# Linear attention in units of one whole load group, with the maxima in the bank of the key-value sums

## The chip, the cores and the metric

The kernel runs on one core of a Trainium2 chip. The metric is the device time of one execution in microseconds (us), from a launch with all inputs in device memory. PE is TensorE, DVE is VectorE, ACT is ScalarE, POOL is GpSimd and SP is SyncE.

## The reference

Three parts follow each other: a linear attention with positive random features, a gated MLP with an RMS norm ahead of it, and a second MLP.

```
scale = 1 / sqrt(sqrt(D))                      # D = 64, m = 128 features
phi(x): proj = x*scale @ omega.T               # q, k, v: batch 4, heads 8, seq 576, D 64
        h = proj - sum((x*scale)^2)/2
        exp(h - max(h)) / sqrt(m)
kv = phi(k).T @ v ;  z = sum(phi(k))           # per batch and head
attn = (phi(q) @ kv) / (phi(q) @ z + 1e-6)
x = attn as 2304 tokens x 512
xn = x / rms(x) * rms_g
x = (silu(xn @ w_gate) * (xn @ w_val)) @ w_out # d_ff 1536
out = silu(x @ w_in) @ w_out2                  # d_ff 2048
```

The MLP weights arrive as float64 words, which the kernel turns into float32 itself.

## The kernel before

A float32 product is made of three passes on TensorE: each operand is split into a high part (a rounded copy, made by ScalarE) and a low part (the rest, a subtraction on VectorE), and `PASS` runs high*high, high*low and low*high.

**Attention.** A load group is 256 rows of four heads of k or q in one tile `x` of 128 partitions x 512 (row pairs, so four heads x two rows = eight columns of 64); a tail group holds the last 64 rows of two batches and is half as wide. There are 32 whole groups and 8 tail groups. A whole group is worked on as two units of four columns, one after the other; with the tails there are 72 units. Each unit runs through the same steps, named here as in the code: `tr` (PE, L586: two transposes into a PSUM buffer `b`), `tr_hi` (ACT, L592) and `tr_lo` (DVE, L595), which split the transposed tile into `hl`, `pj` (PE, L605: six matmuls against `bd`, the features), `mx` (DVE, L620: the maximum over the features of four columns, into `small`), `top` and `nb` (DVE, L626 and L633: the bias of the exponential from the maximum and the squared norms `ns`), and `ex` (ACT, L644: four exponentials into `e`). A k unit then adds its part of the key-value sums (`kv`, PE, L690); after the last one of a batch and a half of the heads VectorE copies the sums to `kvs` (L710). A q unit is transposed again (`fl`, L721, and `ev` on ACT, L727), multiplied with `kvs` (`num`, L736), divided on VectorE (`den`, `rec`, `mu`, L759 to L772), and when a tile of 128 tokens is whole it is normed (`ss` on ACT, `rstd` on POOL, `xn` on DVE, L833), transposed (`xf`, L842) and split into `xs` (`x_hi`, `x_lo`, L851 and L856).

**PSUM.** The eight banks are: one for `small` (maxima and intermediate sums of three units), one for the key-value sums `kv`, and six buffers `b` for everything else.

**Weights.** Each weight tile is loaded into `raw`, decoded in five steps on VectorE and two on POOL, and split (`w_hi`, `w_lo`). The first six and three more are prepared during the attention, the others later.

**The order.** The attention, the weights of the first sweep and the first sweep of the gated MLP over the first three blocks of tokens (`part`, L236, into `b`; `out`, L963) are written as `Op`s with an engine, an estimated duration, dependences and buffers that they claim and free. `run_order` (L413) is a list scheduler: it takes again and again the operation that can start earliest, with `RANK` added to a place in the sequence as priority. So the table `RANK`, the durations and the buffer counts in `SLOTS` set the order in which the instructions stand on each engine; the engines then run their own instructions strictly in that order and wait for each other by semaphores that the framework sets from the tiles that instructions touch. After `run_order`, `stream` writes the rest of the MLPs in a fixed order (L236, L290, L323), and every few microseconds of estimated TensorE work a `tick` puts in the next step of a weight.

Of the kernel before, what the change touches and what calls it, by code (L numbers as in the profile page):

```python
# [20 lines left out]
def kernel(  # L21
# [202 lines left out]
    W_EARLY, GRAIN = 3, 3  # L224
# [152 lines left out]
    class Op:  # L377
# [15 lines left out]
        "ld_om": 41.7, "t_om": -211.5, "s_om": -232.3, "bd_hi": -107.5, "bd_lo": 58.9,  # L393
# [4 lines left out]
        "rstd": -389.4, "xn": 36.2, "xf": -367.8, "x_hi": -48.8, "x_lo": 225.6, "ld_w": 11.5,  # L398
        "w_dec": 310.2, "w_add": 254.1, "w_hi": 67.9, "w_lo": 196.9, "part": 226.4, "tanh": 300.8,
        "silu": -31.9, "glu": 10.3, "h_hi": -176.1, "h_lo": -143.8, "out": 711.2, "ya": -190.5,  # L400
    }
    SLOTS = {
# [68 lines left out]
    small = ps_a.tile([P, SLOTS["nb"], 2 * G], F32, tag="small", name="small", bufs=1)  # L471
# [25 lines left out]
    def k_units(b):  # L497
        for g in range(2):
            for hf in range(2):
                for hp in range(2 * g, 2 * g + 2):  # L500
                    yield "k", b, hf, hp, g
            if b % 2 == 0:
                yield "kt", b, 0, 0, g

    def q_units(b):
        for hf in range(2):
            for hp in range(4):
                yield "q", b, hf, hp, hp // 2
        if b % 2:
            for g in range(2):  # L510
                yield "qt", b - 1, 0, 0, g
# [8 lines left out]
    last_use = {}  # L520
    for i, (kind, b, hf, hp, g) in enumerate(units):
        last_use[kind, b, hf, g] = i
    last_k = max(i for i, u in enumerate(units) if u[0][0] == "k")
# [5 lines left out]
    def add_load(u, i):  # L529
# [42 lines left out]
    def add_unit(i):  # L572
        kind, b, hf, hp, g = units[i]
        u = kind, b, hf, g
        tail = len(kind) == 2
        if u not in ld:
            add_load(u, i)
        w = ld[u]
        st = State()

        def transposes(o):
# [18 lines left out]

        def project(o):
            st.ps = buf(ps_a, [P, G, P], "b", o.slot["b"])
            for j in range(2):
                for n, (a, c) in enumerate(PASS):
                    nc.tensor.matmul(  # L605
                        out=st.ps[:, 2 * j:2 * j + 2, :].rearrange("p h m -> p (h m)"),
                        lhsT=st.hl[:, c, j, :],
                        rhs=bd[:, a, :],
                        start=(n == 0),
                        stop=(n == 2),  # L610
                    )

        pj = Op("pj", "PE", 0.71, project, [lo] + bd_ops, i, ["b", "pjc"], [(tr, "hl")])
        pj_ops.append(pj)

        def maxima(o):
            n = o.slot["nb"]
            st.mx, st.top = small[:, n, 0:G], small[:, n, G:2 * G]
            st.nb = buf(wk, [P, G], "nb", n)
            nc.vector.tensor_reduce(out=st.mx, in_=st.ps, axis=AX.X, op=ALU.max)  # L620
            st.ns = w.ns if tail else w.ns[:, 4 * (hp % 2):4 * (hp % 2) + 4]

        mx = Op("mx", "DVE", 0.6, maxima, [pj], i, ["nb"])
        top = Op(
            "top", "DVE", 0.13,
            lambda o: nc.vector.scalar_tensor_tensor(  # L626
                out=st.top, in0=st.ns, scalar=half, in1=st.mx, op0=ALU.mult, op1=ALU.add
            ),
            [mx, w.nsop], i,
        )  # L630
        nb = Op(
            "nb", "DVE", 0.13,
            lambda o: nc.vector.scalar_tensor_tensor(  # L633
                out=st.nb, in0=st.ns, scalar=half, in1=st.top, op0=ALU.mult, op1=ALU.subtract
            ),
            [top], i, free=[(w.sqop, "ns")] if last_use[u] == i else [],
        )
        res = f"et{g}" if kind == "kt" else "e"

        def exps(o):  # L640
            pool = kp if kind == "kt" else wk
            st.e = buf(pool, [P, G, M], res, o.slot[res])
            for h in range(G):
                nc.scalar.activation(  # L644
                    out=st.e[:, h, :], in_=st.ps[:, h, :], func=AF.Exp, bias=st.nb[:, h:h + 1]
                )

        ex = Op("ex", "ACT", 1.004, exps, [nb], i, [res], [(pj, "b"), (pj, "pjc"), (mx, "nb")])
        if kind[0] == "k":
            add_kv(i, st, ex)  # L650
        else:
            add_q(i, st, ex)

    def add_kv(i, st, ex):
        kind, b, hf, hp, g = units[i]
        u = kind, b, hf, g
        va = vld[u]
        odd = b % 2
        first = kind == "k" and hf == 0 and hp % 2 == 0
        end = (hf == 1 and hp % 2 == 1) if odd else kind == "kt"  # L660
        deps = [ex, va.op, kvprev.get((b, g))]
        free = []
        if kind == "kt":
            ktexp[b, g] = st, ex, va
        else:
            free.append((ex, "e"))
            if last_use[u] == i:
                free.append((va.op, "v"))
# [415 lines left out]
```

## Time and profile before

| | us |
|---|---|
| median of 3 runs (lowest to highest) | 1010.03 (1009.59 to 1011.81) |
| the profiled execution | 1011.63 |
| its span, first to last instruction | 1009.8 |
| PE busy | 992.4 |
| DVE busy | 587.8 |
| ACT busy | 374.6 |
| POOL busy | 282.2 |

The profiled execution took 1.83 us more than its span, and lies 1.60 us above the median. A busy PE is not PE at its peak, because the ends of pipelined matmuls are modelled. The attention takes roughly the first 160 us, the blocks of the first sweep that `run_order` places go on to about 218 us, and the rest is `stream`.

### The profile page before, as it was taken

To read this page: it belongs to the slowest core of one execution; us is meant where nothing else is said; L and a number is where in the kernel's file an instruction comes from. 1 tells how busy PE (TensorE), PEld (TensorE's weight loads), DVE (VectorE), ACT (ScalarE), POOL (GpSimd) and SP (SyncE) were. 2 spreads that over 40 slices of the span, in tenths; PEclk is the share of its full clock that TensorE was granted. 3 is DMA by queue.
4 is the path that set the end of the run, shared out by engine and by line. 5 is a ranking of instruction groups with operands and counts; after the bars stand their busy time and mean duration, and the time that the engine had idled before them with its cause. 6 is when DMAs were issued, how large, how long until landed. Compare 5 with 4: busy or idle time off the path is not lost.

```text
span 1009.8 us, 15330 instructions
## 1 busy us (share of the span) xinstructions
PE 992.4 (98%) x5935; PEld 842.4 (83%) x5935; DVE 587.8 (58%) x1289; ACT 374.6 (37%) x861; POOL 282.2 (28%) x287
## 2 busy tenths in 40 slices
PE   7999998999999999999999999999999999999998
PEld 7988886788888888888888888888888888888887
DVE  7899998837852345676332776443654544535633
ACT  6988895344221112222111334433322322322321
POOL 6756632415520002344000231321411411201300
PEclk9999999999999999999999999999999999999999
DMA  7444211212320002222000120210210210200023
GB/s 196 123 122 131 67 30 42 64 41 84 104 63 1 1 1 64 63 85 83 21 1 1 42 63 22 84 42 5 79 42 6 78 42 22 63 1 21 21 84 105
DMA packets 68729, 55.85 MB, mean 55 GB/s; under 512 B 25648, under 2 KB 62768, under 8 KB 68656
## 3 DMA queue, kind: packets, MB, share of 16 engines
q1 hardware_dynamic: 68656, 54.87, 18.4%
q8 instruction: 47, 0.77, 0.3%
q14 instruction: 26, 0.21, 0.1%
HBM read 50.14 MB, written 4.72 MB: 54 GB/s over the span
## 4 chain that ended last, share of the span: by engine, by line
PE 89%; DVE 7%; issue 1%; POOL 1%; ACT 1%; DMA 1%; SPq 0%; DVEq 0%; ACTq 0%; POOLq 0%
PE g L236 43%; PE y L323 19%; PE y L290 12%; PE b L605 4%; PE b L236 3%; PE kv L690 2%; DVE small L620 2%; PE b L963 2%; PE b L736 1%; PE b L721 1%; PE b L586 1%; DVE hl L595 1%; DVE w L183 1%; POOL m L170 1%; DVE xt L833 1%
## 5 line engine op out<-in xcount | busy, mean ns | idle before, releaser
L236 PE MATMUL g<-xs,w 128*128 128x512 f32 (+1 forms) x2256 | 467.9, 366 | 0.0
L236 PEld LDWEIGHTS g<-xs,w 128*128 128x128 f32 x2256 | 391.2, 188 | 70.1
L170 POOL TENSOR_TENSOR m<-m,raw 128x512 int32<-128x512 int32 x136 | 189.9, 1396 | 612.6 <-issue 442.6
L230 DVE TENSOR_TENSOR h<-s,h 128x512 fp32r<-128x512 f32 (+1 forms) x134 | 96.0, 717 | 185.0 <-ACT h L229 185.0
L323 PE MATMUL y<-w,h 128*128 128x512 f32 (+1 forms) x870 | 200.8, 388 | 0.0
L323 PEld LDWEIGHTS y<-w,h 128*128 128x128 f32 x870 | 162.2, 188 | 33.3
L229 ACT ACTIVATE h<-s 128x512 fp32r<-128x512 f32 (+1 forms) x134 | 78.7, 588 | 191.5 <-DVE s L259 169.5
L290 PE MATMUL y<-h,w 128*128 128x512 f32 (+1 forms) x648 | 135.6, 366 | 0.3 <-DVE w L183 0.3
L290 PEld LDWEIGHTS y<-h,w 128*128 128x128 f32 x648 | 112.1, 189 | 20.5 <-DVE w L183 0.8
L270 ACT ACTIVATE s<-g 128x512 f32<-128x512 f32 (+1 forms) x80 | 44.4, 556 | 171.0 <-PE g L236 170.9
L334 DVE TENSOR_TENSOR ya<-y,ya 128x512 f32<-128x512 f32 (+1 forms) x91 | 62.2, 684 | 57.8 <-PE y L323 56.5
L259 DVE TENSOR_TENSOR s<-s,g 128x512 f32<-128x512 f32 (+1 forms) x54 | 33.8, 627 | 84.8 <-PE g L236 84.8
L301 DVE TENSOR_TENSOR ya<-y,ya 128x512 f32<-128x512 f32 (+1 forms) x80 | 50.2, 635 | 54.3 <-PE y L290 54.1
L180 ACT ACTIVATE w<-m 128x512 fp32r<-128x512 f32 x68 | 42.7, 628 | 102.8 <-POOL m L170 102.8
L644 ACT ACTIVATE e<-b,nb 128x128 f32<-128x128 f32 x272 | 77.5, 395 | 3.7 <-DVE nb L633 3.6
L605 PE MATMUL b<-bd,hl 128*128 128x256 f32 x432 | 69.5, 300 | 1.7 <-DVE hl L595 1.1
L605 PEld LDWEIGHTS b<-bd,hl 128*128 128x128 f32 x432 | 56.8, 192 | 5.4 <-DVE hl L595 2.3
L620 DVE TENSOR_REDUCE small<-b 128x4 f32<-128x512 f32 x72 | 50.2, 697 | 6.2 <-PE b L605 2.2
L253 ACT ACTIVATE s<-g 128x512 f32<-128x512 f32 (+1 forms) x54 | 29.7, 550 | 64.1 <-PE g L236 63.9
L183 DVE TENSOR_TENSOR w<-m,w 128x512 fp32r<-128x512 f32 x68 | 52.9, 779 | 0.1
L545 POOL TENSOR_TENSOR sq<-x 128x512 f32<-128x512 f32 (+1 forms) x40 | 38.9, 982 | 36.2 <-DMA x<-in_q_dram 9.8
L549 POOL TENSOR_TENSOR sq<-sq 128x256 f32<-128x256 f32 (+2 forms) x80 | 44.4, 573 | 2.3
(69 smaller groups left out, 739.7 us busy)
## 6 DMA issues: line engine op xcount, KB each, us to landing
raw<-in_moe_w_out_dram SPq DMA_DIRECT2D x28, 512.0 KB, 3.5
raw<-in_moe_w_in_dram SPq DMA_DIRECT2D x16, 512.0 KB, 3.7
raw<-in_moe_w_gate_dram SPq DMA_DIRECT2D x12, 512.0 KB, 3.6
raw<-in_moe_w_val_dram SPq DMA_DIRECT2D x12, 512.0 KB, 3.5
x<-in_k_dram SPq DMA_DIRECT2D x16, 256.0 KB, 3.4
va<-in_v_dram SPq DMA_DIRECT2D x32, 128.0 KB, 3.3
x<-in_q_dram SPq DMA_DIRECT2D x16, 256.0 KB, 3.0
out_dram<-ya SPq DMA_DIRECT2D x15, 256.0 KB, 2.0
```

Source lines behind the costliest of these rows:

```text
L170: tt(out=mi, in0=mi, in1=(low if step == 5 else high).bitcast(I32), op=ALU.add)
L183: nc.vector.tensor_tensor(out=st.t[:, 1, :], in0=st.m.bitcast(F32), in1=st.t[:, 0, :].bitcast(F32), op=ALU.subtract)
L229: nc.scalar.activation(out=ht[:, 0, :], in_=s, func=AF.Copy)
L230: nc.vector.tensor_tensor(out=ht[:, 1, :], in0=s, in1=ht[:, 0, :].bitcast(F32), op=ALU.subtract)
L236: nc.tensor.matmul(out=ps, lhsT=w[:, a, cc * P:(cc + 1) * P], rhs=xs[j][:, c, cc, :], start=(n == 0), stop=(n == 3 * KC - 1),)
L290: nc.tensor.matmul(out=ps, lhsT=wt[1, "o", f][:, a, d * P:(d + 1) * P], rhs=hs[f][:, c, :], start=(n == 0), stop=(n == nn - 1),)
L301: nc.vector.tensor_tensor(out=y[:, d, :], in0=ps, in1=y[:, d, :], op=ALU.add)
L323: nc.tensor.matmul(out=ps, lhsT=hs[f][:, a, t * P:(t + 1) * P], rhs=wt[2, "p", f][:, c, d0:d1], start=(n == 0), stop=(n == nn - 1),)
L334: nc.vector.tensor_tensor(out=o[:, t, d0:d1], in0=ps, in1=o[:, t, d0:d1], op=ALU.add)
L605: nc.tensor.matmul(out=st.ps[:, 2 * j:2 * j + 2, :].rearrange("p h m -> p (h m)"), lhsT=st.hl[:, c, j, :], rhs=bd[:, a, :], start=(n == 0) ...
L620: nc.vector.tensor_reduce(out=st.mx, in_=st.ps, axis=AX.X, op=ALU.max)
L644: nc.scalar.activation(out=st.e[:, h, :], in_=st.ps[:, h, :], func=AF.Exp, bias=st.nb[:, h:h + 1])
```

## The change

The unit becomes the whole load group. `tr` is four transposes into one buffer `b`, `tr_hi` and `tr_lo` split all eight columns at once, and `top` and `nb` work on eight columns; `pj`, `mx` and `ex` stay as they are, twice for each group (40 groups instead of 72 units for the other steps). Both maxima are there before `top`. A `kv` operation adds the eight columns of a group, after both its exponentials. The maxima move into the bank of the key-value sums: one tile `sums` of 512 words holds the sums in its first 260 and the maxima in its last 48, and a seventh buffer `b` takes the free bank. There are four `x` buffers instead of five, two `hl` instead of three (each twice as wide), two `nmc` instead of one. The square of the norm writes its unused result into the part of `xs` that `x_lo` fills later. The first weight loads are tied to another projection (`GATE`), some durations are changed, and all of `RANK` has new values.

```diff
--- before.py
+++ after.py
-    W_EARLY, GRAIN = 3, 3
+    W_EARLY, GRAIN, GATE = 3, 3, 13
...
-        "ld_v": 152.1, "tr": -174.1, "tr_hi": -646.3, "tr_lo": -622.3, "pj": -75, "mx": 580.3,
...
+        "ld_v": 43, "tr": 112.1, "tr_hi": 191.5, "tr_lo": 4.7, "pj": -40.7, "mx": -1915.3,
...
-        "x": 5, "v": 3, "vt0": 1, "vt1": 1, "sq": 2, "ns": 6, "hl": 3, "b": 6, "pjc": 4, "nb": 3, "e": 3,
-        "et0": 1, "et1": 1, "kv": 1, "kvs": 6, "qT": 2, "nmc": 1, "xt": 2, "rs": 4,
+        "x": 4, "v": 3, "vt0": 1, "vt1": 1, "sq": 2, "ns": 6, "hl": 2, "b": 7, "pjc": 4, "nb": 3, "e": 3,
+        "et0": 1, "et1": 1, "kv": 1, "kvs": 6, "qT": 2, "nmc": 2, "xt": 2, "rs": 4,
...
-    small = ps_a.tile([P, SLOTS["nb"], 2 * G], F32, tag="small", name="small", bufs=1)
+    sums = ps_a.tile([P, 512], F32, tag="sums", name="sums", bufs=1)
+    kv_sum = sums[:, 0:G * (D + 1)].rearrange("p (h d) -> p h d", h=G)
+    small = sums[:, 512 - 4 * G * SLOTS["nb"]:].rearrange("p (n t) -> p n t", n=SLOTS["nb"])
...
-                for hp in range(2 * g, 2 * g + 2):
-                    yield "k", b, hf, hp, g
+                yield "k", b, hf, g
...
+    def add_unit(u, i):
+        kind, b, hf, g = u
         tail = len(kind) == 2
-        if u not in ld:
-            add_load(u, i)
-        w = ld[u]
+        R = 1 if tail else 2
...
-            st.pt = buf(ps_a, [P, 2, P], "b", o.slot["b"])
-            st.hl = buf(wk, [P, 2, 2, P], "hl", o.slot["hl"], F32R)
-            for j in range(2):
-                h0, n = (2 * j, 2) if tail else (2 * (hp % 2) + j, 1)
-                nc.tensor.transpose(
-                    st.pt[:, j, :], w.x[:, h0:h0 + n, :, :].rearrange("p h r d -> p (h r d)"), ident
-                )
-
-        free_x = [(w.op, "x")] if last_use[u] == i else []
-        tr = Op("tr", "PE", 0.218, transposes, [w.op, w.sqop], i - 1, ["b", "hl"], free_x)
-        hi = Op("tr_hi", "ACT", 0.264, lambda o: nc.scalar.activation(out=st.hl[:, 0], in_=st.pt, func=AF.Copy), [tr], i - 0.3)
+            st.pt = buf(ps_a, [P, 2 * R, P], "b", o.slot["b"])
+            st.hl = buf(wk, [P, 2, 4, P], "hl", o.slot["hl"], F32R)
+            for j in range(2 * R):
+                nc.tensor.transpose(st.pt[:, j, :], flat()[:, j * P:(j + 1) * P], ident)
+
+        tr = Op("tr", "PE", 0.109 * 2 * R, transposes, [w.op, w.sqop], i - 1, ["b", "hl"], [(w.op, "x")])
+        hi = Op(
+            "tr_hi", "ACT", 0.25 * R,
+            lambda o: nc.scalar.activation(out=st.hl[:, 0, 0:2 * R], in_=st.pt, func=AF.Copy), [tr], i - 0.3,
+        )
         lo = Op(
-            "tr_lo", "DVE", 0.335,
+            "tr_lo", "DVE", 0.07 + 0.265 * R,
             lambda o: nc.vector.tensor_tensor(
-                out=st.hl[:, 1], in0=st.pt, in1=st.hl[:, 0].bitcast(F32), op=ALU.subtract
+                out=st.hl[:, 1, 0:2 * R], in0=st.pt, in1=st.hl[:, 0, 0:2 * R].bitcast(F32), op=ALU.subtract
...
+            pj = Op("pj", "PE", 0.715, project, [lo] + bd_ops, i, ["b", "pjc"], [(tr, "hl")] if last else [])
+            pjs.append(pj)
+
+            def maxima(o, r=r):
+                if r == 0:
+                    n = o.slot["nb"]
+                    st.mx, st.top = small[:, n, 0:G * R], small[:, n, 2 * G:2 * G + G * R]
+                    st.nb = buf(wk, [P, G * R], "nb", n)
+                nc.vector.tensor_reduce(out=st.mx[:, G * r:G * r + G], in_=st.ps[r], axis=AX.X, op=ALU.max)
+
+            mxs.append(Op("mx", "DVE", 0.64, maxima, [pj] + mxs, i, ["nb"] if r == 0 else []))
...
+            exs.append(Op(
+                "ex", "ACT", 1.004, exps, [nb], i, [res],
+                [(pjs[r], "b"), (pjs[r], "pjc")] + ([(mxs[0], "nb")] if r == R - 1 else []),
+            ))
...
-        deps = [ex, va.op, kvprev.get((b, g))]
+        first = kind == "k" and hf == 0
+        end = hf == 1 if odd else kind == "kt"
+        deps = exs + [va.op, kvprev.get((b, g))]
...
-                acc.ps = buf(ps_a, [P, G, D + 1], "kv", o.slot["kv"])
+                acc.ps = kv_sum
...
+                for n in range(2 * G):
+                    h, r = n // 2, n % 2
+                    jobs.append((h, st.e[n // G][:, n % G, :], va.v[:, h, r, :]))
...
-            junk = wk.tile([P, DM], BF16, tag="junk", name="junk", bufs=1)
...
+            junk = xs[j][:, 1, :, o0:o0 + P]
+            nc.scalar.activation(out=junk, in_=xs_.x[:, r].rearrange("p (c a) d -> p c (a d)", c=KC), func=AF.Square, accum_out=xs_.ss[:, r:r + 1])
...
+            add_weight(job, n, [pj_ops[GATE + n]])
```

What the scheduler makes of it is shown at three places. The names: `hl`, `ns`, `nb`, `e` and `b` are buffers of the steps above, the number behind an underscore tells one use of a buffer from another, and `waits` names the engines (or DMA queues) whose semaphores the instruction waits for.

First, VectorE in the middle of the attention. Before, with a split, a maximum, a `top` and a `nb` for each four columns:

```order
L595 TENSOR_TENSOR hl0_1620<-b5_1619,hl0_1620 128x256 [waits Activation_49]
L626 SCALAR_TENSOR_TENSOR small_98<-ns0_1148,small_98 128x4 [waits DVE_49]
L558 TENSOR_REDUCE ns1_1610<-sq0_1609 128x4 [waits Pool_49]
L633 SCALAR_TENSOR_TENSOR nb2_1629<-ns0_1148,small_98 128x4 [waits DVE_49]
L620 TENSOR_REDUCE small_98<-b2_1632 128x4 [waits DVE_49,PE_49]
L595 TENSOR_TENSOR hl1_1647<-b0_1646,hl1_1647 128x256 [waits Activation_49]
L626 SCALAR_TENSOR_TENSOR small_98<-ns2_1321,small_98 128x4 [waits DVE_49]
L620 TENSOR_REDUCE small_98<-b1_1652 128x4 [waits DVE_49,PE_49]
L633 SCALAR_TENSOR_TENSOR nb1_1666<-ns2_1321,small_98 128x4 [waits DVE_49]
```

Now, for two whole groups:

```order
L625 TENSOR_REDUCE sums_98<-b4_1270 128x4 [waits PE_49]
L167 TENSOR_SCALAR m0_1132<-m0_1132 128x512
L625 TENSOR_REDUCE sums_98<-b2_1288 128x4 [waits DVE_49,PE_49]
L625 TENSOR_REDUCE sums_98<-b6_1302 128x4 [waits DVE_49,PE_49]
L631 SCALAR_TENSOR_TENSOR sums_98<-ns4_881,sums_98 128x8 [waits DVE_49]
L625 TENSOR_REDUCE sums_98<-b0_1313 128x4 [waits DVE_49,PE_49]
L638 SCALAR_TENSOR_TENSOR nb1_1300<-ns4_881,sums_98 128x8 [waits DVE_49]
L631 SCALAR_TENSOR_TENSOR sums_98<-ns5_993,sums_98 128x8 [waits DVE_49,PE_49]
L843 SCALAR_TENSOR_TENSOR xt1_1013<-xt1_1013,rstd1_1240,g_sb_88 128x512 [waits Activation_49,Pool_49]
L560 TENSOR_REDUCE ns3_1282<-sq1_1281 128x8 [waits Pool_49]
L638 SCALAR_TENSOR_TENSOR nb2_1320<-ns5_993,sums_98 128x8 [waits DVE_49]
L596 TENSOR_TENSOR hl0_1325<-b5_1324,hl0_1325 128x512 [waits Activation_49]
```

One `top` and one `nb` now serve eight columns. The second `top` (L631, on `ns5_993`) waits for PE although all that it reads was written by VectorE.

Second, TensorE at the same place, now:

```order
L750 MATMUL b3_1340<-kvs2_878,qT1_1278 64x65 [waits Activation_49]
L750 MATMUL b3_1340<-kvs2_878,qT1_1278 64x65 x7
L699 MATMUL sums_98<-va2_101,e2_1256 64x65 [waits DVE_49]
L699 MATMUL sums_98<-va2_101,e2_1256 64x65 x7
L699 MATMUL sums_98<-va2_101,e0_1295 64x65 x8
L852 MATMUL b4_1388<-ident_82,xt1_1013 128x128 [waits DVE_49,PE_49,Activation_49]
```

The 16 matmuls of a `kv` operation stand together, and the first waits for VectorE, where the last instruction on `sums` ahead of it is the `nb` of the rows above (`nb1_1300`); the `top` that follows there waits for the last of the 16. Of all first matmuls of `kv`, 18 wait for VectorE now and one did before; the `top` and `nb` that wait for PE are 11 of 80 now and none of 144 before.

Third, TensorE at the end of the attention. Before, around the last exponentials that are flipped ahead of the dense block work (`xs0` is the first block of tokens, `w0_0` and `w0_2` its first two weights):

```order
L236 MATMUL b1_3211<-xs0_90,w0_0_1833 128x512 x6
L721 MATMUL b3_3226<-ident_82,e1_3205 128x128 x4
L236 MATMUL b1_3211<-xs0_90,w0_0_1833 128x512 x3
L721 MATMUL b2_3243<-ident_82,e2_3221 128x128 x4
L236 MATMUL b1_3211<-xs0_90,w0_0_1833 128x512 x3
L736 MATMUL b5_3252<-kvs0_2499,qT0_3131 64x65 x8
L736 MATMUL b4_3277<-kvs0_2499,qT1_3193 64x65 x8
L842 MATMUL b5_3289<-ident_82,xt1_3062 128x128 x4
```

Now, at the same point:

```order
L236 MATMUL b2_2956<-xs0_90,w0_2_2912 128x512 x6
L608 MATMUL b6_2986<-bd_87,hl1_2926 128x256 x6
L732 MATMUL b4_2994<-ident_82,e2_2963 128x128 x4
L732 MATMUL b0_3007<-ident_82,e0_2980 128x128 x4
L236 MATMUL b2_2956<-xs0_90,w0_2_2912 128x512 x3
L852 MATMUL b5_3019<-ident_82,xt0_2589 128x128 x4
L732 MATMUL b4_3027<-ident_82,e1_2999 128x128 x4
L236 MATMUL b2_2956<-xs0_90,w0_2_2912 128x512 x3
L852 MATMUL b0_3045<-ident_82,xt0_2589 128x128 x4
L236 MATMUL b5_3051<-xs0_90,w0_1_2484 128x512 x3
L732 MATMUL b6_3062<-ident_82,e2_3038 128x128 x4
```

The twelve matmuls of the first product (`w0_0`) stand more than a hundred rows earlier now, between projections, and those of the second (`w0_2`) where the first stood: 27 matmuls of the block (12 + 12 + 3) stand ahead of the last flip of exponentials (L732 on `e2_3038`) now, and nine (6 + 3) stood ahead of the last one (L721 on `e2_3221`) before.

## Rows read from the trace of the kernel before

**Rows 1.** Windows by stage: busy us (instructions) of each engine, granted clock, DMA share, GB/s.
```profile
25.00:150.00 125.00, 120.34 (x1569) 108.72 (x1567) 116.64 (x394) 111.00 (x363) 78.12 (x114) 1.00 0.36 96
150.00:162.00 12.00, 10.12 (x78) 8.39 (x73) 9.84 (x24) 8.46 (x25) 3.55 (x4) 0.86 0.08 16
162.00:218.20 56.20, 54.29 (x322) 43.56 (x322) 39.47 (x81) 24.43 (x44) 17.80 (x16) 1.00 0.20 63
218.20:264.40 46.20, 45.87 (x237) 39.03 (x236) 32.46 (x57) 18.48 (x32) 20.14 (x14) 1.00 0.22 69
```

**Rows 2.** Chain that ended last: start us, us, what.
```profile
216.80 1.38 PE b L963 x6
218.18 13.73 PE g L236 x72
...
264.32 6.66 PE y L290 x28
```

**Rows 3.** Waits of PE from 218 us on: us in total, times, longest.
```profile
PE y L290 <- DVE w L183: 0.3, 1, 0.3
```

**Rows 4.** Waits of DVE and of ACT, 25 to 150 us.
```profile
DVE small L620 <- PE b L605: 1.6, 4, 0.5
...
ACT hl L592 <- PE b L586: 6.1, 14, 2.0
ACT qT L727 <- PE b L736: 3.9, 6, 1.1
```

**Rows 5.** Groups of DVE by form, 0 to 162 us: busy us, mean ns; idle before.
```profile
L620 DVE TENSOR_REDUCE small<-b 128x4 f32<-128x512 f32 x72 | 50.2, 697 | 6.2 <-PE b L605 2.2
L595 DVE TENSOR_TENSOR hl<-b,hl 128x256 fp32r<-128x256 f32 x72 | 29.4, 418 | 1.1 <-ACT hl L592 0.6
...
L626 DVE SCALAR_TENSOR_TENSOR small<-ns,small 128x4 f32<-128x4 f32 x72 | 11.5, 160 | 0.6
...
L633 DVE SCALAR_TENSOR_TENSOR nb<-ns,small 128x4 f32<-128x4 f32 x72 | 10.7, 152 | 1.4
L856 DVE TENSOR_TENSOR xs<-b,xs 128x512 fp32r<-128x512 f32 x13 | 8.7, 682 | 0.1
```

**Rows 6.** Timeline of DVE, 60 to 70 us: start us, us, what.
```profile
62.97 0.68 DVE L856 TENSOR_TENSOR xs<-b,xs 128x512 fp32r<-128x512 f32 x1
63.57 0.17 DVE L762 RECIPROCAL rd<-rd 128x4 f32<-128x4 f32 x1
...
66.29 0.16 DVE L633 SCALAR_TENSOR_TENSOR nb<-ns,small 128x4 f32<-128x4 f32 x1
66.36 0.42 DVE L595 TENSOR_TENSOR hl<-b,hl 128x256 fp32r<-128x256 f32 x1
66.70 0.16 DVE L626 SCALAR_TENSOR_TENSOR small<-ns,small 128x4 f32<-128x4 f32 x1
66.96 0.70 DVE L620 TENSOR_REDUCE small<-b 128x4 f32<-128x512 f32 x1
67.69 0.16 DVE L633 SCALAR_TENSOR_TENSOR nb<-ns,small 128x4 f32<-128x4 f32 x1
```

**Rows 7.** Timeline of PE, 130 to 160 us.
```profile
136.21 0.69 PE L690 MATMUL kv<-va,e 128*64 128x65 f32 x16
136.82 1.10 PE L690 MATMUL kv<-vat,et 64*128 64x65 f32 x8
...
139.32 0.97 PE L605 MATMUL b<-bd,hl 128*128 128x256 f32 x6
...
155.23 0.94 PE L736 MATMUL b<-kvs,qT 128*64 128x65 f32 x16 [1.54 <-DVE xs L856]
```

**Rows 8.** Timeline of DVE, 136 to 141 us.
```profile
140.33 0.70 DVE L620 TENSOR_REDUCE small<-b 128x4 f32<-128x512 f32 x1 [0.51 <-PE b L605]
```

**Rows 9.** Timeline of PE, 12 to 17 us, and of DVE there.
```profile
13.65 0.97 PE L605 MATMUL b<-bd,hl 128*128 128x256 f32 x6 [0.43 <-DVE hl L595]
...
13.18 0.75 DVE L595 TENSOR_TENSOR hl<-b,hl 128x256 fp32r<-128x256 f32 x2
```

More of the change, by code (lines that the diff above doesn't have):

```diff
@@ L518 @@
             qs, ks = qs[1:], ks[1:]
[L520 to L523, printed above, removed]
+    place, at = [], 0
+    for u in units:
+        place.append(at)
+        at += 1 if len(u[0]) == 2 else 2
+    last_k = max(n for n, u in zip(place, units) if u[0][0] == "k")
     ld, vld, kvfirst, kvprev, kvcopy, ktexp, xtop = {}, {}, {}, {}, {}, {}, {}
@@ L599, in add_unit @@
         )
[L601 to L623, printed above, removed]
+        st.ps, st.e, pjs, mxs, exs = {}, {}, [], [], []
@@ L624, in add_unit @@
+        pj_ops.append(pjs[0])
         top = Op(
-            "top", "DVE", 0.13,
+            "top", "DVE", 0.11,
             lambda o: nc.vector.scalar_tensor_tensor(
-                out=st.top, in0=st.ns, scalar=half, in1=st.mx, op0=ALU.mult, op1=ALU.add
+                out=st.top, in0=w.ns, scalar=half, in1=st.mx, op0=ALU.mult, op1=ALU.add
             ),
-            [mx, w.nsop], i,
+            mxs + [w.nsop], i,
         )
         nb = Op(
-            "nb", "DVE", 0.13,
+            "nb", "DVE", 0.11,
@@ L633, in add_unit @@
             lambda o: nc.vector.scalar_tensor_tensor(
-                out=st.nb, in0=st.ns, scalar=half, in1=st.top, op0=ALU.mult, op1=ALU.subtract
+                out=st.nb, in0=w.ns, scalar=half, in1=st.top, op0=ALU.mult, op1=ALU.subtract
             ),
-            [top], i, free=[(w.sqop, "ns")] if last_use[u] == i else [],
+            [top], i, free=[(w.sqop, "ns")],
         )
         res = f"et{g}" if kind == "kt" else "e"
[L640 to L646, printed above, removed]
@@ L648, in add_unit, with exps @@
-        ex = Op("ex", "ACT", 1.004, exps, [nb], i, [res], [(pj, "b"), (pj, "pjc"), (mx, "nb")])
+        for r in range(R):
+            def exps(o, r=r):
+                pool = kp if kind == "kt" else wk
+                st.e[r] = buf(pool, [P, G, M], res, o.slot[res])
+                for h in range(G):
+                    nc.scalar.activation(
+                        out=st.e[r][:, h, :], in_=st.ps[r][:, h, :], func=AF.Exp,
+                        bias=st.nb[:, G * r + h:G * r + h + 1],
+                    )
+            exs.append(Op(
+                "ex", "ACT", 1.004, exps, [nb], i, [res],
+                [(pjs[r], "b"), (pjs[r], "pjc")] + ([(mxs[0], "nb")] if r == R - 1 else []),
+            ))
@@ L649, in add_unit, with add_kv @@
         if kind[0] == "k":
-            add_kv(i, st, ex)
+            add_kv(u, i, st, exs)
         else:
[L652 to L656, printed above, removed]
+            for r in range(R):
+                add_q(u, i, st, r, exs[r])
+    def add_kv(u, i, st, exs):
+        kind, b, hf, g = u
         va = vld[u]
         odd = b % 2
-        first = kind == "k" and hf == 0 and hp % 2 == 0
-        end = (hf == 1 and hp % 2 == 1) if odd else kind == "kt"
-        deps = [ex, va.op, kvprev.get((b, g))]
+        first = kind == "k" and hf == 0
+        end = hf == 1 if odd else kind == "kt"
+        deps = exs + [va.op, kvprev.get((b, g))]
@@ L699, in accumulate @@
                 open_early()
-        o = Op("kv", "PE", 0.9 if kind == "kt" else 1.4 if odd and end else 0.47, accumulate, deps, i - 1, ["kv"] if first else [], free)
+        o = Op("kv", "PE", 0.95 if kind == "kt" else 1.95 if odd and end else 0.93, accumulate, deps, i - 1, ["kv"] if first else [], free)
         kvprev[b, g] = o
@@ L790, in add_q, with spot @@
                 add_norm(i, key, r, r == R - 1)
+    def spot(key, r):
+        kind, b, hf = key
+        j, n = divmod(tidx["m" if kind == "q" else "t", b, hf, r], TB)
+        return j, n * P
     def add_norm(i, key, r, last):
@@ L835, in scale_x @@
             )
-        xn = Op("xn", "DVE", 0.61, scale_x, [rs, g_op], i, free=[(xs_.sq[0], "rs")] if last else [], port=True)
+        xn = Op("xn", "DVE", 0.69, scale_x, [rs, g_op], i, free=[(xs_.sq[0], "rs")] if last else [], port=True)
         def flip_x(o):
```

102 lines of the change are left out of this document (53 added, 49 removed), and 5 rows, old and new, of the table RANK.

## The prediction

> **What bounds the kernel now.** I read the chain of waits first, then the windows by stage, then who waits for whom in the stage that changes, and last single instructions. From 218.18 us on the chain runs through TensorE's matmuls of the fixed stream [rows 2], and from there to the end TensorE waits once, for 0.3 us, at 264 us for the low half of a weight [rows 3]. The windows say the same: 45.87 of 46.20 us busy behind 218 us [rows 1]. The change touches nothing behind that point, and the weight that TensorE waits for at 264 us hangs on vector work that itself starts from TensorE's product at 232 us, so it moves along. So the end moves by what the start of the stream at 218.18 us moves by.
>
> Ahead of it are two stages. From 162 to 218 us TensorE is busy 54.29 of 56.20 us [rows 1]: block work back to back. Ahead of 162 us it is the attention, where every engine looks full: from 25 to 150 us PE 120, DVE 117 and ACT 111 of 125 us. The waits tell them apart [rows 4]. VectorE waits for TensorE (the row shown, the largest) 1.6 us in all of that stretch; ScalarE waits for TensorE's transposes 6.1 us and for the numerators 3.9 us. TensorE's 120 us count stretched matmuls. I read it as VectorE setting the pace. The 6.8 us in which VectorE is neither busy nor in that wait are gaps between instructions: an instruction that needs the one ahead of it starts about 0.03 us after its end (the maximum at 66.96 us ends at 67.66, the next starts at 67.69), one that doesn't starts 0.08 us before its end (66.36 + 0.42, next 66.70) [rows 6].
>
> **The change part by part.** I sum against the span of the profiled execution, 1009.8 us; its run took 1.83 us more, and the median, 1010.03 us, is what I apply the difference to.
>
> *Fewer `top` and `nb`.* 72 of each become 40: 32 fewer of 160 ns and 32 fewer of 152 ns [rows 5], that is 32 x 0.312 = 10.0 us of VectorE. From start to start such an instruction costs from 0.07 us (66.29 to 66.36) to 0.26 us (66.70 to 66.96) [rows 6], so the bounds are 64 x 0.07 = 4.5 and 64 x 0.26 = 16.6 us. I take 10.0, since about half of them are of each kind.
>
> *One split for eight columns.* 64 narrow `tr_lo` become 32 wide ones (the eight of the tails stay). The trace has no wide `tr_lo`; the nearest row is `x_lo`, the same subtraction from PSUM on 128x512. Two narrow ones cost 2 x 0.34 us from start to start, a wide one 0.60 (62.97 to 63.57) [rows 6]: 32 x 0.08 = 2.6 us. Bounds: nothing, and 32 x (2 x 0.418 - 0.682) = 4.9 us by durations [rows 5]. Together VectorE loses 12.6 us of work, between 4.5 and 21.5.
>
> Here the Trainium skill would give more: "VectorE: DVE Perf Modes", section "The DRAIN you can't avoid", says that each vector instruction waits until the pipe of the one ahead is empty, and that semaphores between them cost nothing. By that rule the whole durations come back, 10.0 + 4.9 = 14.9 us instead of 12.6. The rows disagree: independent instructions overlap by 0.08 us, and a dependent one pays 0.11 us more [rows 6].
>
> *The shared bank.* Before, `small` and the sums lay in two banks, and no `top` or `nb` waited for TensorE. Now the framework treats the bank as one thing: `kv` waits for the last vector instruction on it, and the next vector instruction on it waits for the end of `kv`. In the new order I find 18 `kv` groups with such a wait on the way in, and 14 of them hold a following `mx`, `top` or `nb` on the way out. The trace has no such round trip, so I build it. TensorE starts 0.05 us after a vector instruction that it waits for (the first of the two at 13.18 us ends at 13.60, TensorE starts at 13.65) [rows 9]; 16 matmuls of `kv` take 0.69 us and the tail ones (eight in 1.10 us, now four) about half of 1.10 us [rows 7]; VectorE starts 0.04 us after the end of TensorE's work (139.32 + 0.97, start 140.33) [rows 7, 8]. That is 0.78 us for a group of 16, 1.25 us for one with a tail, which starts 0.61 us behind. Nine of the fourteen are of the first kind, four of the second, one is a tail alone (0.64): 12.7 us if VectorE has nothing else to do. In five of the fourteen a wide split stands between (0.60 each), in others norms, quotients' first steps or a second split, together 4.8 us of cover. That leaves 7.9 us. Bounds: nothing, if the sums are long done when VectorE gets there, and 12.7. I take the full 7.9, because VectorE is the engine that the others wait for, so that TensorE stands ready when the bank comes free. Queued behind the waiting instruction are the splits that feed the next projections and the maxima that ScalarE's exponentials need.
>
> *A longer first fill.* The first bias now needs a second maximum (0.70 us [rows 6]) and a wide split, 0.682 - 0.418 = 0.26 us more on VectorE [rows 5] and about as much on ScalarE: +1.2 us, once; bounds nothing and 2.
>
> *Block work pulled forward.* 27 matmuls of the first block lie ahead of the last flip of exponentials, nine before. At 0.23 us each (six in 1.38 [rows 2]) 18 x 0.23 = 4.1 us leave the dense stage from 162 to 218 us and go where TensorE has room. But then the low half of the last early weight, which stands only about 18 us of vector work behind that flip, can come late for `out`, so I take half, -2.0 us; bounds 0 and -4.1.
>
> *The rest.* ScalarE's wide split saves it a little and VectorE's relief is what it must follow; the unused squares go into another buffer at the same width, the four `x` buffers instead of five come free after one `tr` instead of two, and the seventh `b` holds what the merged bank gave. I cost these at nothing: what covers them is ScalarE's waiting of 10 us in 125 [rows 4]. If that is used up, the second rival below holds.
>
> Sum: -12.6 + 7.9 + 1.2 - 2.0 = -5.5 us: span 1004.3, median 1004.5 us.
>
> **The rivals.** *The bank costs nothing* (0.14): where `kv` runs long before VectorE's next instruction on the bank, nothing is left of the 7.9 us: -13.4 us, 996.6 us. For it speaks that the scheduler puts `kv` where it finds it free; against it that it knows nothing of the bank.
>
> *ScalarE takes over, or latency does* (0.20). A k group now holds two of three `e` buffers until its `kv`, and `kv` now waits for VectorE. If each of the 16 whole k groups holds ScalarE back by 0.3 us, 4.8 us of the gain go, -0.7 us: 1009.3 us, no change. ScalarE's 111 busy us in 125 and only some 10 us of waiting, against a relief of 12.6 x 125/160 = 9.8 us in that stretch, speak for it [rows 1, 4].
>
> *The bank costs more than the work saved* (0.20). If nothing stands in for the round trips (12.7 us), and TensorE, which runs its instructions in order, also stands still behind each of the 18 groups for half a maximum (0.35 us, 6.3 us in all) with projections and flips queued behind, and with no block work gained: -12.6 + 12.7 + 6.3 + 1.2 = +7.6 us, 1017.6 us. It decides against the change from the point at which the bank costs more than 12.6 + 2.0 - 1.2 = 13.4 us, 0.74 us for each of 18 groups. The Trainium skill speaks for this side: "PSUM — Partial Sum Buffer", section "Terms", says that no two of TensorE, VectorE and ScalarE may access one bank within the same partition in one cycle. No run here shows it yet; by it these waits are no slip of the framework and cannot be dropped.
>
> **How the numbers follow.** The forecast, that VectorE's relief reaches the end with the bank's price taken off, has 0.46 and reaches from 1001 to 1008 us. A difference of 0.2%, 2 us, is about what a measurement of this kernel can tell from none. Faster is the forecast and the first rival, 0.60; the second rival is the same, 0.20; the third slower, 0.20. The range takes in most of the first rival and the third up to some 3 us over the old time: 997 to 1013 us.
>
> TensorE's clock may add to either side: between 150 and 162 us the granted clock averages 0.86, that is 3.4 us at the lower of its two levels (1.2 GHz), and TensorE had stood idle for 1.54 us until 155.23 us just before [rows 1, 7]. If that gap closes, 1.7 us come back; if two open, 1.7 us go.
>
> **What would show it right or wrong.** Right: the stream's first matmul of line 236 on a g tile starts near 213 us; VectorE's `top` and `nb` at about 155 ns x40 each; the wide `tr_lo` near 0.68 us; rows in which VectorE's `mx`, `top` or `nb` wait for TensorE's `kv` line, some 5 to 9 us in all; dense TensorE from there to the end with one short wait. Wrong: the `kv` round trips near nothing (then faster) or over 13 us (then slower); ScalarE waiting less than 3 us in the middle while VectorE waits for its exponentials or splits; a wait of `out` for the last early weight of several us; a second stretch at 1.2 GHz.

## The result and the profile after

The change makes the kernel slower: 1024.51 us median of 4 runs (1023.51 to 1024.72) against 1010.92 of 4 (1009.59 to 1011.86), a ratio of 1.0134 with an interval of 1.0116 to 1.0151. The prediction, 1004.5 us and faster, was wrong, and the time lies over its range. The profiled spans, 1021.7 and 1009.8 us, differ by 11.9 us.

First the chain that ended last, in the trace after (start us, us, what), to be held against [rows 2], and TensorE's waits from 229 us on against [rows 3].

```profile
229.88 13.78 PE g L236 x72
...
276.08 6.65 PE y L290 x28
```

```profile
PE y L290 <- DVE w L183: 0.3, 1, 0.3
```

The stream starts 11.7 us later (218.18 before) and is the same behind that point, down to its one wait. All of the loss lies ahead of it. The windows by stage (columns as in [rows 1]):

```profile
25.00:150.00 125.00, 107.58 (x1398) 98.38 (x1400) 102.62 (x275) 95.22 (x295) 73.93 (x104) 0.99 0.37 98
150.00:162.00 12.00, 10.29 (x146) 9.26 (x143) 8.99 (x29) 8.76 (x28) 3.59 (x8) 0.99 0.06 13
162.00:175.00 13.00, 12.71 (x158) 11.70 (x158) 11.70 (x37) 11.02 (x32) 2.75 (x3) 0.88 0.13 44
175.00:229.50 54.50, 54.37 (x317) 44.83 (x315) 40.49 (x85) 28.69 (x65) 20.23 (x20) 1.00 0.19 58
```

From 25 to 150 us all three engines are less busy than before: TensorE 107.6 instead of 120.3, VectorE 102.6 instead of 116.6, ScalarE 95.2 instead of 111.0. When all become idler at once, none has become the bound: they stand in each other's way. The groups of VectorE by form say that the work itself became smaller as forecast (0 to 230 us; busy us, mean ns; idle before, as in [rows 5]):

```profile
L625 DVE TENSOR_REDUCE sums<-b 128x4 f32<-128x512 f32 x72 | 50.1, 696 | 14.4 <-PE b L608 6.5 <-PE sums L699 5.2
L596 DVE TENSOR_TENSOR hl<-b,hl 128x512 fp32r<-128x512 f32 x32 | 21.3, 682 | 0.0
...
L631 DVE SCALAR_TENSOR_TENSOR sums<-ns,sums 128x8 f32<-128x8 f32 x32 | 5.4, 169 | 8.0 <-PE sums L699 7.2
...
L638 DVE SCALAR_TENSOR_TENSOR nb<-ns,sums 128x8 f32<-128x8 f32 x32 | 5.0, 158 | 5.8 <-PE sums L699 5.3
```

With the eight of the tails (2.5 us) `top` and `nb` take 12.9 us instead of 22.2. But behind the bars stand new waits, most of them for TensorE's key-value matmuls (L699). The view of that one line shows both sides: what TensorE's queues stood idle for in front of it, and who waited for it.

```profile
its engine sat idle before it (us, times) until:
  DVE nb L638: 4.8, 5
  DVE sums L625: 3.9, 6
  DVE rd L763: 2.4, 4
  DVE sums L631: 1.9, 5
  issue: 0.3, 2
who waited for it (us, times):
  DVE sums L631: 7.2, 5
  DVE nb L638: 6.3, 6
  DVE sums L625: 5.2, 4
  PEld b L750: 2.9, 2
  PEld b L608: 1.1, 1
  DVE kvs L719: 0.5, 1
```

VectorE waits 19.2 us for key-value sums at 16 places, and TensorE's queues stood still 13.0 us in front of them: weight loads and matmuls counted apart, so that most of it is counted twice; the matmuls alone stood still 5.5 us. Of the four engine rows of the first list three are instructions on the bank. The fourth, `rd`, is not, but in the round trip below the maximum at 66.33 us, which is on the bank, ends at 67.02 us, 0.05 us before the group starts. Before, that line waited 0.2 us for VectorE, and nobody waited for it. One such round trip (timeline, 66 to 71 us):

```profile
66.33 0.69 DVE L625 TENSOR_REDUCE sums<-b 128x4 f32<-128x512 f32 x1
...
66.93 0.22 DVE L763 TENSOR_SCALAR rd<-b 128x4 f32<-128x4 f32 x2
...
67.07 1.15 PE L699 MATMUL sums<-va,e 128*64 128x65 f32 x32 [0.68 <-DVE rd L763]
...
68.15 1.10 PE L699 MATMUL sums<-vat,et 64*128 64x65 f32 x8
...
69.29 0.17 DVE L631 SCALAR_TENSOR_TENSOR sums<-ns,sums 128x8 f32<-128x8 f32 x1 [2.15 <-PE sums L699]
...
69.58 0.76 DVE L776 TENSOR_TENSOR xt<-b,rd 128x256 f32<-128x256 f32 x2
...
70.15 0.63 PE L732 MATMUL b<-ident,e 128*128 128x128 f32 x4 [0.28 <-DVE xt L776]
...
70.37 0.64 ACT L813 ACTIVATE xs<-xt 128x512 fp32r<-128x512 f32 x1 [2.20 <-DVE xt L776]
```

The matmuls of a whole group (32 rows, 1.15 us) and those of a tail (8 rows, 1.10 us) stand back to back, 2.2 us in all; a `top` that has nothing to do with them waits 2.15 us, and behind it on VectorE's queue wait the quotients, for which ScalarE stands still 2.20 us and TensorE's next flip 0.28.

### The profile page after: what moved, and what is told of

Same layout as the page of the kernel before. It is cut to its first block, busy times and chain, and to the rows that moved or that the text cites. A ratio compares the mean times of both kernels' runs of the same rounds, so it can differ in the third digit from the quotient of the medians.

```text
span 1021.7 us, 15226 instructions
## 1 busy us (share of the span) xinstructions
PE 990.1 (97%) x5935; PEld 843.7 (83%) x5935; DVE 582.2 (57%) x1193; ACT 370.7 (36%) x829; POOL 282.4 (28%) x287
## 4 chain that ended last, share of the span: by engine, by line
PE 88%; DVE 8%; ACT 1%; issue 1%; DMA 1%; POOL 0%; SPq 0%; DVEq 0%; ACTq 0%; POOLq 0%
PE g L236 43%; PE y L323 19%; PE y L290 12%; PE b L608 3%; PE b L236 3%; PE sums L699 3%; DVE sums L625 2%; PE b L973 2%; PE b L750 1%; PE b L732 1%; DVE xt L843 1%; DVE hl L596 1%; PE b L587 1%; PE b L852 1%; DVE w L183 1%
## 5 line engine op out<-in xcount | busy, mean ns | idle before, releaser
L236 PE MATMUL g<-xs,w 128*128 128x512 f32 (+1 forms) x2256 | 468.0, 366 | 0.0
L236 PEld LDWEIGHTS g<-xs,w 128*128 128x128 f32 x2256 | 391.1, 188 | 70.0
L608 PE MATMUL b<-bd,hl 128*128 128x256 f32 x432 | 67.0, 300 | 3.7 <-DVE hl L596 3.1
L625 DVE TENSOR_REDUCE sums<-b 128x4 f32<-128x512 f32 x72 | 50.1, 696 | 14.4 <-PE b L608 6.5
L551 POOL TENSOR_TENSOR sq<-sq 128x128 f32<-128x128 f32 (+2 forms) x80 | 45.1, 591 | 0.6
```

The lines of the kernel that those rows point to most:

```text
L236: nc.tensor.matmul(out=ps, lhsT=w[:, a, cc * P:(cc + 1) * P], rhs=xs[j][:, c, cc, :], start=(n == 0), stop=(n == 3 * KC - 1),)
L608: nc.tensor.matmul(out=st.ps[r][:, 2 * j:2 * j + 2, :].rearrange("p h m -> p (h m)"), lhsT=st.hl[:, c, 2 * r + j, :], rhs=bd[:, a, :], sta ...
L625: nc.vector.tensor_reduce(out=st.mx[:, G * r:G * r + G], in_=st.ps[r], axis=AX.X, op=ALU.max)
```

## The experiments

Theory: at the order that the planner made, the shared bank's waits cost about all of the loss. Rivals: the wide units (two maxima before one bias, more held by one unit), the refitted ranks with the later omega load, and the size of the gain.

**Sharing taken away, alone.** Every engine's order stays; the maxima leave the bank for SBUF.

```
-    small = sums[:, 512 - 4 * G * SLOTS["nb"]:]...
+    small = wk.tile([P, SLOTS["nb"], 4 * G], F32, ...)
```

> The changed kernel with maxima and top in SBUF instead of in the bank of the key-value sums; every engine's order stays. Bank theory: the 18.7 us that VectorE waits for TensorE in front of top, nb and mx of that bank (15 waits) and TensorE's 5.5 us before key-value matmuls go away, and 12 to 18 us of them reach the end: 1006 to 1013 us. Rival (coarse units: two projections before one bias, ScalarE late): the waits only move to another engine and the time stays within 3 us of the changed kernel's 1024.5. Rival (refitted ranks, omega loaded third): also within 3 us of 1024.5.

Measured 1002.41 us, ratio to before 0.992 (0.9907 to 0.9932): 22.1 us under the changed kernel, 8.0 under the kernel before. The sharing is the cause, and it cost more than its visible waits. The other parts of the change (wide units, ranks, buffer counts, `GATE`, the place of the unused squares) are still in this kernel. VectorE is filled again, and its waits from 0 to 185 us hold none for the sums:

```profile
25.00:150.00 125.00, 119.33 (x1632) 110.79 (x1631) 118.86 (x326) 108.98 (x342) 77.52 (x114) 1.00 0.39 103
```

```profile
DVE small L625 <- PE b L608: 4.9, 13, 0.6
DVE bd L1018 <- ACT bd L1016: 4.8, 1, 4.8
```

**The control: the kernel before with maxima in SBUF.**

> The kernel before with maxima and top in SBUF, a control of what the other place costs by itself; the order stays. All theories: the bank of maxima was private to VectorE, so no wait goes away and the time is within 2 us of 1010.9; what it differs by is the price of SBUF operands in top and nb (102 of each) and is taken off the result of the units with SBUF maxima.

1020.48 us, 1.0102 (1.0087 to 1.0118). All theories missed this: SBUF is no free place. `top` lasts 318 ns instead of 160 and `nb` 297 instead of 152 (72 of each, not 102 as in the expectation: 21.6 us more).

```profile
L626 DVE SCALAR_TENSOR_TENSOR small<-ns,small 128x4 f32<-128x4 f32 x72 | 22.6, 318 | 0.3
L633 DVE SCALAR_TENSOR_TENSOR nb<-ns,small 128x4 f32<-128x4 f32 x72 | 21.2, 297 | 0.2
```

The timeline (VectorE and GpSimd, 69 to 74 us) shows why:

```profile
71.16 1.04 POOL L545 TENSOR_TENSOR sq<-x 128x512 f32<-128x512 f32 x1
71.58 0.63 DVE L633 SCALAR_TENSOR_TENSOR nb<-ns,small 128x4 f32<-128x4 f32 x1
...
73.29 0.15 DVE L633 SCALAR_TENSOR_TENSOR nb<-ns,small 128x4 f32<-128x4 f32 x1
```

An `nb` that starts inside a GpSimd operation ends with it (72.20 and 72.21); one with no GpSimd operation beside it lasts 0.15 us. The Trainium skill has the rule, in "SBUF — State Buffer", section "Who interferes with whom": a vector instruction with two SBUF inputs contends with a GpSimd instruction that reads SBUF, and the later one stands still. The trace agrees: the `nb` that came later does not end before the GpSimd operation. So the first experiment's 22.1 us is a net figure: it paid this price as well (its 80 `top` and `nb` took 24.2 us instead of 12.9).

**Sharing added, alone**, to the kernel before (order unchanged).

```
+    sums = ps_a.tile([P, 512], F32, ...)
...
+    small = sums[:, 512 - 2 * G * SLOTS["nb"]:]...
...
-                acc.ps = buf(ps_a, [P, G, D + 1], "kv", ...)
+                acc.ps = kv_sum
```

> The kernel before, its units, ranks and six b banks kept, with maxima and key-value sums in one bank; the order stays. Bank theory: 36 key-value groups and 102 chains of mx, top and nb on one bank give at least as many round trips as in the changed kernel, half as long: plus 8 to 18 us, 1019 to 1029 us. Rivals (coarse units; ranks): nothing of theirs is in it, within 2 us of 1010.9.

1028.12 us, 1.0176 (1.0162 to 1.019): +17.7. The line of its key-value matmuls, who waited for it:

```profile
  DVE nb L635: 10.5, 14
  DVE sums L622: 8.2, 10
  DVE sums L628: 4.0, 8
  PEld b L738: 1.7, 2
```

22.7 us at 32 places, 0.71 us each: shorter groups make more and shorter trips. At 16 places of 1.2 us the changed kernel is little better off.

**Two banks, wide units.** One b bank less, the planner makes the order anew; then the same with the old ranks.

```
-    ... "hl": 2, "b": 7, ...
+    ... "hl": 2, "b": 6, ...
...
+    small = ps_a.tile([P, SLOTS["nb"], 4 * G], F32, ...)
```

> The changed kernel with maxima and key-value sums in two banks again, so six b banks instead of seven; the planner makes its order anew under six. Bank theory: as with maxima in SBUF, 1006 to 1014 us, or some us more where the seventh b bank was worth something. Rivals (coarse units; ranks): within 3 us of 1024.5, or above.

> The units of a load group with maxima and key-value sums in two banks, six b banks as before, and the rank table of the kernel before, which was made for six: the wide units alone. Theory that the wide units save VectorE's work and that two banks keep it (VectorE's top and nb in PSUM take 12.6 us instead of 22.2, the wide hl 24.9 instead of 29.4): 14 us less of VectorE's work, of which about 8 reach the end: 999 to 1006 us. Rival (one bias for two projections comes too late for ScalarE, and banks stay held longer): 1010 to 1018 us, as with the new ranks (1014.9).

1014.90 us (1.0041, 1.0028 to 1.0053) and 1018.00 (1.008, 1.0065 to 1.0095). The expected 999 to 1006 for the second was missed by 12 us: wide units with a bank of their own for the maxima are still slower than before, at these orders.

**The ranks and the omega load.** The changed kernel with the old rank table; and the SBUF version with omega second on SyncE (`"ld_om": -273.3`).

> The changed kernel (units of a load group, shared bank, seven b banks) with the rank table of the kernel before; the omega load is then second on SyncE. Bank theory: the ranks hardly matter, since neither table was made by a plan that knows the bank, so the bank's waits stay and the time is within 6 us of the changed kernel's 1024.5. Rival (the refit itself costs time): 1010 to 1016 us.

> Maxima in SBUF as in the first experiment (1002.4 us), and the rank of the omega load changed so that it goes out second on SyncE, as in the kernel before. Omega theory: the first matmul starts 1.0 us earlier (4.0 us instead of 5.1), VectorE and ScalarE are the filled engines from there, so about 1 us reaches the end: 1001 to 1002 us. Rival (the first second load of x, now 0.5 us later, takes its place, or the order behind it shifts): no change that can be measured, within 1 us of 1002.4, or above.

1021.17 us: the refit is at most 3.3 us of the loss. 1002.43 us: the first matmul did start at 3.97 instead of 5.08 us, and nothing of it reaches the end.

**A planner that knows the bank**, with the change's ranks.

```
+                    if o.bank:
+                        other = "DVE" if eng == "PE" else "PE"
+                        s = max(s, held[other] + LAT[other])
```

> The changed kernel, its shared bank and ranks kept, with a planner that knows the bank: a maximum, top, nb or copy of the sums starts only after the key-value group given out before it has ended, and the other way round, so that the planner gives VectorE other work meanwhile. Theory that the waits cost by being unplanned: VectorE's 18.7 us of waits for key-value sums fall under 8 us and the time to 1008 to 1017 us. Rival (the round trips cost however they are planned, since VectorE has nothing else that is ready and the biases come late for ScalarE): 1018 to 1025 us.

1019.98 us. VectorE's waits for the sums fall from 19.2 to 3.9 us, yet the time by only 4.5: by the planner's own account (table below) unseen waits became planned delays. Seeing the waits go was not enough.

**More banks, less VectorE work, a planner that knows the port.** The kernel before with SBUF maxima and seven b banks; `top` and `nb` as three GpSimd operations; `port=True` on `top` and `nb`.

> The kernel before with maxima in SBUF (1020.5 us in the second experiment) and seven b banks instead of six, planned anew; its units of four columns and its ranks stay. Theory that the seventh bank carries the gain of the version with SBUF maxima: 1002 to 1010 us. Rival (the gain is the wide units' saved VectorE work): 1015 to 1022 us.

> Wide units, maxima in SBUF, and top and nb on GpSimd (three small operations a unit there, 120 in all) instead of VectorE (80 that took 24.2 us with SBUF operands). Theory that VectorE's work is what bounds the stage: 24 us less of it, GpSimd has room (13 of 25 us busy), so 8 to 15 us reach the end: 987 to 995 us. Rival (GpSimd's queue: a bias stands behind squares of 1.0 us and behind the weights' integer work of 1.35 us, and ScalarE's exponentials wait for it): 1002 to 1015 us.

> Wide units with maxima in SBUF (1002.4 us), and a planner that counts top and nb among the operations that exclude GpSimd's, so that it starts them where GpSimd is free and its own work later. Theory that top and nb last 290 ns instead of 160 because GpSimd's operations block them: their mean falls under 220 ns and the time to 994 to 1000 us. Rival (the order made so is later by what it gives way, or the plan's times of GpSimd are too far off to help): 1000 to 1008 us.

1037.17, 1009.46 (0.9991, 0.9982 to 1.0001) and 1030.50 us. The first settles nothing about the seventh bank: its ranks were made for six. The second is the plainest miss: 24 us of VectorE's work taken away cost 7 us. The likely reason is that the bias now stands in GpSimd's queue: ScalarE waits 9.6 us for it, and waited 3.8 us for VectorE's `nb` in the first experiment. The third shortens `top` to 241 and `nb` to 219 ns and loses 28 us by the order that makes room for it.

These orders differ in much, so I asked what the kernel's planner itself says: the end that it gives the last operation of the stage, a number of the program and no measurement.

| kernel | planner's end | measured | difference |
|---|---|---|---|
| before | 208.1 | 1010.4 | 802.3 |
| two banks, new ranks | 214.4 | 1014.9 | 800.5 |
| two banks, old ranks | 221.3 | 1018.0 | 796.7 |
| bank known | 218.7 | 1020.0 | 801.3 |
| port known | 231.6 | 1030.5 | 798.9 |
| **changed** | 202.2 | 1024.5 | **822.3** |
| changed, old ranks | 208.3 | 1021.2 | **812.9** |
| before, shared bank | 208.1 | 1028.1 | **820.0** |
| before, SBUF maxima | 208.1 | 1020.5 | **812.4** |
| before, SBUF maxima, seven `b` | 223.4 | 1037.2 | **813.7** |
| changed, SBUF maxima | 202.2 | 1002.4 | 800.2 |

Where the planner knows the waits, the time is its end and some 797 to 802 us (the GpSimd version, whose small operations it plans too long, 790.6); where it doesn't, it is 10 to 20 us more. The last row's planner doesn't know the price of SBUF, and it doesn't show. By its own account the change was worth 208.1 - 202.2 = 5.9 us, close to the 5.5 that I predicted. Open was then whether wide units and a shared bank can pay in an order that is made for them. Four kernels with ranks fitted anew by that end alone, and two that move the maxima only:

> Wide units, two banks, six b banks (1014.9 us with the new ranks, 1018.0 with the old) with ranks fitted anew to this very plan: its planner's own last operation ends at 205.4 us instead of 214.4; that of the kernel before ends at 208.1 with 1010.4 measured. Theory that the wide units cost only where the order was made without them: the measured time follows the plan, 1005 to 1009 us. Rival (wide units make biases late and hold banks whatever the order): 1012 to 1018 us.

> Wide units, shared bank, seven b banks, the planner that knows the bank (1020.0 us with the new ranks) with ranks fitted anew to that plan: its planner's last operation ends at 204.3 us instead of 218.7. Theory that the bank's waits cost because the order was made without them: the waits of VectorE for key-value sums fall from 18.7 us to under 6 and the time to 1004 to 1010 us. Rival (the round trips cost however they are planned): 1015 to 1022 us.

> The two-bank kernel with six b banks (1014.9 us) with maxima and top in SBUF instead of their bank, every engine's order the same: the price of the SBUF operands alone. Theory that top and nb then stand behind GpSimd's operations: their mean rises from 165 to about 290 ns, VectorE's work by some 10 us, of which half reaches the end: 1018 to 1023 us. Rival (VectorE has idle time in this order, 15 to 20 us before the stream): 1014 to 1016 us.

> Wide units, maxima in SBUF, seven b banks (1002.4 us) with 0.17 us instead of 0.11 for top and nb in the planner and ranks fitted anew to it. Theory that an order made for the longer operations is better than the one that came with the change: 997 to 1001 us. Rival (the order of the change already fits, its plan ends at 202.2 us without the longer operations, the new one at 205.1 with them): 1002 to 1006 us.

> The kernel before with its ranks fitted anew in the same way and for as long as those of the wide units: its plan ends at 206.6 us instead of 208.1. Theory that the wide units are what gains in the refitted kernels: within 2 us of the kernel before, 1008 to 1011 us. Rival (the fitting alone does it): 1002 to 1006 us.

> The shared-bank kernel with the bank in its plan and refitted ranks (1003.7 us), with maxima and top in SBUF and every engine's order the same, so that no bank is shared. Theory that a plan which knows the bank leaves next to nothing of its price (1.9 us of VectorE's waits, 3.1 of TensorE's): 1001 to 1005 us. Rival (the bank still costs behind the waits that are seen): 996 to 1000 us.

| kernel | planner's end | measured | ratio to before |
|---|---|---|---|
| two banks, refitted | 205.4 | 1003.49 | 0.9931 (0.9916 to 0.9946) |
| shared bank known, refitted | 204.3 | 1003.70 | 0.9933 (0.9918 to 0.9948) |
| two banks, new ranks, SBUF maxima | 214.4 | 1014.32 | 1.0039 (1.0026 to 1.0051) |
| SBUF maxima, refitted | 205.1 | 1002.52 | 0.992 (0.9905 to 0.9935) |
| before, refitted | 206.6 | 1008.24 | 0.998 (0.9971 to 0.9989) |
| shared bank's order, SBUF maxima | 204.3 | 1006.87 | 0.9968 (0.9956 to 0.9979) |

The refitted shared bank is 20.8 us faster than the changed kernel, with the same units, buffers and bank. Its key-value line (who waited for it):

```profile
  DVE sums L640: 1.9, 2
  ACT e L659: 1.1, 3
  DVE nb L647: 0.7, 1
```

2.6 us of VectorE's waits instead of 19.2. Taking the sharing away at that order (last row) makes it 3.2 us slower, the SBUF price without a gain; its 1006.87 us lie over both expected ranges. The seventh buffer that sharing frees shows no gain either: two banks with six buffers, refitted, are as fast (1003.49 us). The fitting alone gives the kernel before 2.3 us; the wide units in fitted orders are 4.5 to 5.7 us ahead of that. SBUF maxima cost nothing at the order of the two-bank kernel (1014.32 against 1014.90): there VectorE seems to have room (busy 111.2 of the 125 us from 25 to 150, where the kernel before has 116.6).

## Why the prediction was wrong

- *Nothing changes behind the stream's start*: right. Its start moved 11.7 us, the span 11.9.
- *Fewer `top` and `nb`, -10.0 of work*: right, -9.3. *Wide split, -2.6*: by durations 29.4 [rows 5] to 24.6 us with the tails' 3.3, -4.8.
- ***The shared bank, +7.9: the step that failed.*** Shown: 22.1 us net by taking it away at the same order, 17.7 by adding it to the kernel before. The kinds and the number of trips were nearly right: nine behind a whole group, four behind a group with a tail, one behind a tail alone; two more came, both behind a tail. What I had wrong is how long a group's matmuls last. I took the row of 16 matmuls in 0.69 us [rows 7] for the 16 of a new group. But the trace holds two rows for each of these matmuls, and that row was a unit of four columns; its trip of 0.78 us is near the 0.71 us of the narrow groups in *Sharing added*. The rows of the line (least, median and largest ns), first before, then after:

```profile
L690 PE MATMUL kv<-va,e x512: 219/222/271, 11.5 to 136.7; 128*64 128x65 f32 x171
```

```profile
L699 PE MATMUL sums<-va,e x512: 219/222/271, 16.8 to 158.1; 128*64 128x65 f32 x171
L699 PE MATMUL sums<-vat,et x64: 272/272/322, 23.8 to 159.0; 64*128 64x65 f32 x64
```

  The 16 whole groups of k have 16 matmuls each in the program, 256, and 512 rows: 32 rows a group, 1.15 us. In the same way eight rows in 1.10 us are the four matmuls of one tail, now as before. With my own 0.05 and 0.04 us around it a trip costs 1.24 us instead of 0.78, with a tail 2.27 instead of 1.25 (the tail starts 1.08 us behind), and 1.19 for a tail instead of 0.64: 21.4 us instead of 12.7 for the fourteen, 23.8 for all sixteen. VectorE waited 19.2 us, so 4.6 us were covered, and the 4.8 us of cover that I took off were about right. 21.4 - 4.8 = 16.6 in place of 7.9 turns my sum from -5.5 to +3.2 us, 1013.3 us: slower, and still 11 us short. Toward the rest the trace shows a wait that I put at nothing, because I held that TensorE stands ready: its matmuls stood still 5.5 us in front of the groups. And ScalarE's waits for biases grew from 3.6 to 13.0 us (0 to 185 us; before, then after):

```profile
ACT e L644 <- DVE nb L633: 3.6, 5, 1.2
```

```profile
ACT e L650 <- DVE nb L638: 13.0, 12, 2.9
```

  How much of the 11 us each of these is, no run shows.
- *VectorE sets the pace, so its work returns one for one*: too simple. 21.6 us more on VectorE in the kernel before cost 10 us; some 13 more in the two-bank kernel (25.4 us in `top` and `nb` instead of 12.6) nothing; 24 less with the bias on GpSimd lost 7. What pays is work taken away in an order that can use it.
- *First fill, +1.2*: the first exponentials start at 14.00 us, 4.1 later than before. The version with SBUF maxima starts them at 14.63 and is 8 us faster in the end, so this is no cause of the loss.
- *Block work pulled forward, -2.0*: the count came as forecast; what it is worth stays open. 18 rows of the block (L236) stand ahead of the end of the last projection now and none before. From there to the start of the stream pass 52.9 us instead of 66.1 (152.07 to 218.18 before, 176.94 to 229.88 after), 53.1 in the SBUF version, so more than this work has left the stretch. But the last projection itself ends later than before in both faster kernels compared (155.6 us in the SBUF version, 160.0 with two refitted banks), so the shorter stretch alone is no gain.
- *A second stretch at 1.2 GHz*: came (last section); the span's granted clock is 0.997 (0.993 to 0.995 in the three other executions), which is 3 us lost, 0.998 before and 1.000 in the SBUF version.

The rival *the bank costs more than the work saved* had mechanism and side right; its price of 19.0 us was still 3 short, and its deciding point, 13.4 us, was passed. It has the same misread row in it: with 21.4 instead of 12.7 us it comes to 1026.3 us, 1.8 over the measured time. That closeness is in part luck, since it lets nothing be covered and 4.6 us were.

## What to carry to other kernels

A planned order is only as good as the waits that its planner knows: a buffer that is merged adds dependencies to each pair of its users, and unless the planner sees them every such pair is a lottery. Hold the planner's own end of a stage against the measured one for the kernel before and after; when they stop moving together, a wait is missing, and adding it pays in full only with the priorities fitted again. And where an operand is moved to save a bank or a wait, look who shares the port of its new place. Before a row of a trace is used as the price of an operation, hold its count against the program's own.

## What was not expected of the hardware

Two SBUF operands on VectorE beside a busy GpSimd double the mean time of an operation on 128x4 values (318 against 160 ns). The longest took 1.23 us: it started at 149.94 us, inside two GpSimd operations that last from 148.47 to 151.15, and ended at 151.17.

The trace holds 512 rows for the 256 matmuls of the whole k groups and 64 for the 32 of the tails, but one row for each matmul of the projections (432).

TensorE's clock fell to its lower level right behind a wait in the changed kernel: a timeline row of TensorE and windows of 1 us (granted clock third from the end):

```profile
102.66 1.15 PE L750 MATMUL b<-kvs,qT 128*64 128x65 f32 x32 [3.06 <-DVE xt L776]
```

```profile
105.00:106.00 1.00, 1.00 (x5) 0.90 (x5) 0.20 (x1) 0.00 (x0) 1.00 (x2) 0.50 0.00 0
...
108.00:109.00 1.00, 1.00 (x9) 0.83 (x8) 0.79 (x2) 1.00 (x5) 0.87 (x3) 1.00 0.00 0
```

It had idled 3.06 us until 102.66. The clock stayed full until 103 us, averaged 0.90 in the next microsecond, was 0.50 (1.2 GHz) from 104 and full again at 108; between 161 and 166 us the same followed a wait of 1.18 us.
